# Three moves in a fused attention and hard-swish kernel: one square to ScalarE, one sum of g behind a unit, one square behind an exponential

## The chip, the cores and the metric

The kernel runs on one core of a Trainium2 chip. The metric is the device time of one execution in microseconds (us); the profile's own count, the span, begins with the first instruction of the program and ends with the last. The engines have short names: PE is TensorE (matrix products), DVE is VectorE, ACT is ScalarE, POOL is GpSimd, SP is SyncE, which here only issues DMAs. Each engine works through its own queue in order and waits for the others by semaphores.

## The reference

The computation is cosine attention, followed by a two-layer network with a hard-swish between the layers.

```python
# q, k, v: (8, 12, 448, 64) float32; w_in: (768, 2048); w_out: (2048, 768)
q_n = q / (norm(q, axis=-1) + 1e-06)
k_n = k / (norm(k, axis=-1) + 1e-06)
scores = q_n @ k_n.T / tau
attn = exp(scores - max(scores))
attn = attn / (sum(attn) + 1e-09)
x = (attn @ v).transpose(0, 2, 1, 3).reshape(3584, 768)
h = x @ w_in
g = h * clip(h + 3, 0, 6) / 6
out = g @ w_out                       # float32
```

## The kernel before, in words

The 96 heads are worked on two at a time: 48 pairs, numbered 0 to 47, six to a batch. Raw queries and keys come in "items": item j holds the queries or the keys of two pairs, so that items 2d and 2d+1 belong to pairs 2d and 2d+1. From item 14 on, an even item holds keys and an odd one queries; item 18 is thus the keys of pairs 18 and 19, and item 21 the queries of pairs 20 and 21. An item is 128 partitions by 896 numbers in float32.

What happens to an item: LQ loads it (a DMA on SP's queue), SQ squares it, RE sums the squares (VectorE), NO makes the reciprocals of the norms with four small instructions on ScalarE, NM multiplies them in and casts to bf16 (GpSimd or VectorE), XD transposes by a DMA, and CK and CS copy the keys to where the scores read them (CK on VectorE; CS, from pair 14 on, as two small copies "km" on GpSimd). An SQ may run on ScalarE (letter a, line 227), on GpSimd (p) or on VectorE (v, both line 229). Two buffers hold squares, so the square of item j waits for the reduce of item j-2.

What happens to a pair i: SC.i.g makes four groups of scores. Groups 0 to 2 are two matmuls into two banks of PSUM each (line 445), group 3 is one. EX.i.g takes the exponentials on ScalarE, one instruction for each bank (line 463), and so frees the bank. VA.i.g multiplies by the values (line 486) into the tile PV; FI.i divides by the sums on VectorE (lines 506 and 507) and frees PV for the next pair; XB or XP transposes the result by DMA into xT.

The network is cut into units. A "first product" F is six matmuls (line 597) into one bank; then comes a relu on ScalarE (line 613, it writes one of three tiles u), and a product on VectorE (line 619) that writes g and frees the bank. The second product is done in blocks by a scheme with seven products in place of eight (units such as 5a.3: product 5 of block pair 3, line 762), which need sums of blocks of g (g_sum, line 740, VectorE) and sums of blocks of w_out (weight_sums, WS, line 710, on VectorE or GpSimd). A copy or an addition then reads the bank (lines 781, 787, 799, 810, 819), and GpSimd does additions on what was copied out (lines 791 to 803).

Scores, first products and second products all take their banks in turn from one ring of six: M0, M1, Y, Z, M2, M3. A unit can't start before the sixth-last user's bank was read out.

The order of all engines' work is written by hand. Up to pair 17 it is the list PLAN: a text of steps, each of which puts instructions at the end of the queues of the engines that it uses. U issues the next unit's matmuls, UA its ScalarE step, UV its VectorE step, UP its GpSimd step; W issues the next DMA of weights from GpSimd's queue. From pair 18 on there is one turn for each pair, with its units in TURNS; "+6.3" stands for the sum that product 6 of block pair 3 needs. In a turn, each unit's steps on ScalarE and VectorE follow its matmuls at once; the reduce RE of item i+5 follows the last unit.

The steps that the change touches stand here. In PLAN's line 51, SQ.19 on ScalarE and SQ.18 on GpSimd follow each other; behind them on GpSimd come the two copies of CS.14, then WS.6.p.0 and WS.7.p.0; on VectorE comes WS.1.v.0, which waits for the second of four DMAs of w_out. In PLAN's line 58, SQ.21 on ScalarE stands between EX.16.2 and EX.16.3. In TURNS, turn 29 has four first products, a sum and a product unit; in turn 30, product 2.3 and its sum, and in turn 31, product 6.3, come later.

Of the kernel before, what the change touches and what calls it, by code (L numbers as in the profile page):

```python
# [60 lines left out]
]  # L61
# [3 lines left out]
def kernel(  # L65
# [773 lines left out]
    def products(text):  # L839
# [17 lines left out]
        26: "F 5a.2 4.2 F 2.2",  # L857
        27: "F F 1.2 F 6.2",
        28: "F F 7.2 3.3",
        29: "F F F +6.3 F 5a.3",  # L860
        30: "4.3 F F 2.3 +1.3",
        31: "1.3 F F 6.3 7.3",
        32: "3.4 F F F 5a.4",
# [156 lines left out]
    SC = [psum_s.tile([128, 2, 512], FP32, name=f"SC{n}", tag=f"SC{n}") for n in range(2)]  # L1020
# [118 lines left out]
```

## Time and profile before

| what | value |
|---|---|
| median of three runs | 403.48 us (402.41, 403.48, 406.3) |
| the profiled execution's own time | 403.63 us |
| its span | 401.8 us |
| PE busy | 392.5 us, 98% |
| DVE, ACT, POOL busy | 297.2, 274.5, 248.2 us |
| granted TensorE clock | 1.00 in every stretch |

How to read it: times in the timeline are microseconds from the span's start; each row has the start, the length, the engine, the line of the kernel, the operation and its tiles ("written <- read"), how many instructions it merges, and in brackets how long the engine stood idle before it and what released it. A matmul's record overlaps with its successor's. An instruction's record starts when its engine takes it up; time in which it is blocked further on is part of its length. In the trace, line 51's squares stand at 81.87 (ScalarE) and 82.19 (GpSimd), line 58's at 105.91; the scores of turn 18 begin near 112, those of turn 29 at 192.07 and those of turn 30 at 199.73.

### The profile page before, as it was taken

What the parts mean: (1) busy time and instruction counts of PE and PEld (TensorE: products, weight loads), DVE (VectorE), ACT (ScalarE), POOL (GpSimd) and SP (SyncE); (2) the same over time, 40 slices, a digit from 0 to 9 for tenths busy, and PEclk for the clock granted to TensorE, in tenths of its full rate; (3) what the DMA queues carried; (4) which work ended last, traced back from release to release, by engine and by line L of the source; (5) the groups of instructions that cost most, each with busy time, mean ns of one, the idle gap of its engine ahead of it and who ended that gap; (6) DMA issues with size and microseconds to landing.
All of it is one profiled execution on the core that took longest, in us unless ns stands there. A gap on an engine that the chain in (4) does not pass through costs nothing.

```text
span 401.8 us, 9650 instructions
## 1 busy us (share of the span) xinstructions
PE 392.5 (98%) x3669; PEld 230.9 (57%) x3669; DVE 297.2 (74%) x519; ACT 274.5 (68%) x629; POOL 248.2 (62%) x241
## 2 busy tenths in 40 slices
PE   7999999999999999999999999999999999999996
PEld 5666565545565555555555655555655656555563
DVE  6897688999986697758877767778786566455663
ACT  6899998768997677676776767677677574224230
POOL 7899665591746879698498569839936304201060
PEclk9999999999999999999999999999999999999999
DMA  8999988999479997694866697687665222320143
GB/s 289 293 245 254 232 162 191 246 148 234 97 174 213 192 214 176 145 222 116 208 169 169 171 194 171 155 182 209 124 120 92 46 67 57 74 56 20 29 92 97
DMA packets 92365, 63.73 MB, mean 159 GB/s; under 512 B 56096, under 2 KB 91552, under 8 KB 92320
## 3 DMA queue, kind: packets, MB, share of 16 engines
q1 hardware_dynamic: 87408, 56.45, 60.8%
q0 software_dynamic: 4512, 6.29, 9.4%
q8 instruction: 28, 0.46, 0.5%
q10 hardware_dynamic: 400, 0.39, 0.3%
q14 instruction: 17, 0.14, 0.1%
HBM read 45.61 MB, written 11.01 MB: 141 GB/s over the span
## 4 chain that ended last, share of the span: by engine, by line
PE 77%; DVE 7%; DMA 4%; POOL 4%; issue 3%; ACT 3%; SPq 0%; POOLq 0%; DVEq 0%; ACTq 0%
PE M L597 20%; PE M L762 19%; PE PV L486 10%; PE Y L762 6%; PE Z L762 5%; PE Y L597 5%; PE M L445 5%; PE Z L597 5%; DMA w_out_sb<-in_moe_w_out_dram 2%; DMA big<-in_q_dram 2%; POOL nrm L297 2%; DVE gT L619 2%; POOL big L229 1%; DVE w_sum L710 1%; PE Z L445 1%
## 5 line engine op out<-in xcount | busy, mean ns | idle before, releaser
L597 PE MATMUL M<-xT,w_in_sb 128*128 128x448 bf16 x528 | 111.2, 353 | 0.2 <-ACT at L463 0.2
L597 PEld LDWEIGHTS <-w_in_sb 128*128 128x128 bf16 x768 | 72.4, 98 | 64.3 <-issue 3.1
L463 ACT ACTIVATE at<-M 128x448 bf16<-128x448 f32 x195 | 98.0, 571 | 13.4 <-PE M L445 10.9
L297 POOL TENSOR_TENSOR nrm<-big,r 128x896 bf16<-128x896 f32 (+1 forms) x46 | 76.6, 1671 | 14.4 <-ACT r L260 7.1
L229 POOL TENSOR_TENSOR big<-big 128x896 f32<-128x896 f32 (+3 forms) x41 | 63.3, 1549 | 13.9 <-DVE n L241 5.4
L613 ACT ACTIVATE u<-M 128x448 bf16<-128x448 f32 x88 | 49.3, 561 | 31.3 <-PE M L597 27.8
L486 PEld LDWEIGHTS <-at 128*128 128x128 bf16 (+1 forms) x1536 | 53.9, 97 | 23.3 <-issue 14.4
L619 DVE SCALAR_TENSOR_TENSOR gT<-u,M 128x448 bf16<-128x448 bf16 x75 | 45.8, 617 | 26.0 <-ACT u L613 25.7
L486 PE MATMUL PV<-vx,at 128*128 128x65 bf16 (+1 forms) x1536 | 63.5, 194 | 0.6 <-DVE on L507 0.2
L241 DVE TENSOR_REDUCE n<-big 128x14 f32<-128x896 f32 (+1 forms) x50 | 51.7, 1040 | 2.5 <-POOL big L229 1.5
L762 PEld LDWEIGHTS <-gT 128*128 128x128 bf16 x352 | 33.9, 98 | 23.8 <-issue 0.2
L762 PE MATMUL M<-w_out_sb,gT 128*128 128x384 bf16 x248 | 45.2, 326 | 0.0
L762 PEld LDWEIGHTS <-gs 128*128 128x128 bf16 x312 | 30.1, 98 | 20.8 <-issue 0.6
L791 POOL TENSOR_TENSOR big<-big 128x384 f32<-128x384 f32 x14 | 14.9, 1062 | 36.0 <-ACT big L810 35.9
L402 POOL COPY km<-tT 64x128 bf16<-64x128 bf16 x34 | 13.3, 391 | 38.4 <-DMA tT<-nrm 9.3
L445 PE MATMUL M<-tT,kz 64*128 64x448 bf16 (+1 forms) x172 | 33.5, 351 | 1.2 <-DVE gT L619 0.9
L507 DVE TENSOR_TENSOR on<-PV,rc 128x512 bf16<-128x512 f32 x48 | 33.2, 691 | 1.7
L803 POOL TENSOR_TENSOR o<-o,big 128x384 f32<-128x384 f32 x12 | 12.6, 1056 | 30.6 <-ACT o L799 21.1
L463 ACT ACTIVATE at<-Z 128x448 bf16<-128x448 f32 x52 | 29.5, 567 | 2.0 <-PE M L445 1.8
L463 ACT ACTIVATE at<-Y 128x448 bf16<-128x448 f32 x47 | 26.7, 568 | 4.6 <-PE Z L445 4.3
L597 PE MATMUL Y<-xT,w_in_sb 128*128 128x448 bf16 x132 | 28.7, 353 | 0.0
L762 PE MATMUL M<-w_sum,gs 128*128 128x384 bf16 (+1 forms) x160 | 28.5, 322 | 0.0
(128 smaller groups left out, 581.8 us busy)
## 6 DMA issues: line engine op xcount, KB each, us to landing
big<-in_k_dram SPq DMA_DIRECT2D x24, 448.0 KB, 4.8
big<-in_q_dram SPq DMA_DIRECT2D x24, 448.0 KB, 4.3
out_dram<-o SPq DMA_DIRECT2D x107, 96.0 KB, 2.2
big<-in_v_dram SPq DMA_DIRECT2D x48, 128.0 KB, 4.1
big<-in_v_dram SPq DMA_DIRECT2D x48, 96.0 KB, 4.4
w_out_sb<-in_moe_w_out_dram POOLq DMA_DIRECT2D x4, 768.0 KB, 9.5
w_in_sb<-in_moe_w_in_dram POOLq DMA_DIRECT2D x4, 384.0 KB, 8.3
w_in_sb<-in_moe_w_in_dram POOLq DMA_DIRECT2D x2, 768.0 KB, 10.8
```

The source lines that it names most:

```text
L229: engines[e].tensor_tensor(out=o, in0=i, in1=i, op=ALU.mult)
L241: nc.vector.tensor_reduce(out=n2s[d % 2][:, j % 2, c], in_=sq[:, :, :, :].rearrange("p g c d -> p (g c) d")[:, c, :], axis=AX.X, op=ALU.add,)
L297: engines[e].tensor_tensor(out=nrm[:, :, g, :].rearrange("p c g d -> p g c d"), in0=raw_of[j][:, g, :, :], in1=rs[d % 2][3][:, j % 2, :] . ...
L445: nc.tensor.matmul(o, ks, qt[rows], start=True, stop=True)
L463: nc.scalar.activation(out=o, in_=x, func=AF.Exp, scale=inv_tau)
L486: nc.tensor.matmul(pv_out(j, h), at[rows, n, q_cols(i // HP, j)], vt[rows, 3 + h if name == "M" else 5 * h + int(name[1]), :], start=(name ...
L507: nc.vector.tensor_tensor(out=on[:, :, :, :].rearrange("p j h d -> p h j d"), in0=pv4[:, :, :, 0:D], in1=rc[:, :, :].to_broadcast([128, 2, ...
L597: nc.tensor.matmul(ps[:, 0:S], w_in_sb[:, cc, fc * 128 : (fc + 1) * 128], x[:, cc, 0:S], start=(cc == 0), stop=(cc == CC - 1),)
L613: nc.scalar.activation(out=u[:, :], in_=ps[:, 0:S], func=AF.Relu, bias=0.5, scale=1.0 / 6.0)
L619: nc.vector.scalar_tensor_tensor(out=g[:, fc, c0 : c0 + S], in0=u[:, :], scalar=1.0, in1=ps[:, 0:S], op0=ALU.min, op1=ALU.mult,)
L762: nc.tensor.matmul(m, lhs[:, c, :], rhs[:, c, c0 : c0 + width], start=(base is None and c == 0), stop=(c == KC - 1), skip_group_check=True,)
L791: nc.gpsimd.tensor_tensor(out=e, in0=d, in1=e, op=ALU.add)
```

## The change

Three edits, each in a text that orders the work. The square of item 18 is issued on ScalarE, right behind that of item 19, where it was issued on GpSimd. In turn 29, the sum for product 6.3 follows the fourth first product, where it followed the third. The square of item 21, on ScalarE before and after, follows EX.16.3, where it followed EX.16.2. No instruction is added or taken away beyond the square's change of engine.

```diff
-    "... XD.17 U W U UA UA SQ.19.a.0.7 SQ.18.p.0.7 U CS.14.v WS.1.v.0 UV UV",
+    "... XD.17 U W U UA UA SQ.19.a.0.7 SQ.18.a.0.7 U CS.14.v WS.1.v.0 UV UV",
...
-    "VA.15.1 VA.15.2 EX.16.2 SQ.21.a.0.7 SC.17.0 VA.15.3.h SC.17.1 EX.16.3 FI.15 U VA.16.0 EX.17.0 VA.16.1 UV",
+    "VA.15.1 VA.15.2 EX.16.2 SC.17.0 VA.15.3.h SC.17.1 EX.16.3 SQ.21.a.0.7 FI.15 U VA.16.0 EX.17.0 VA.16.1 UV",
...
-        29: "F F F +6.3 F 5a.3",
+        29: "F F F F +6.3 5a.3",
```

2 rows, old and new, of the table PLAN are left out of this document.

## The prediction

> **What bounds the kernel now.** I read the page's first lines, then the busy time by stretches of 20 us, then the chain of waits in order of time, and last the timeline of each engine at the places that the change touches.
>
> ```profile
> span 401.8 us, 9650 instructions
> PE 392.5 (98%) x3669; PEld 230.9 (57%) x3669; DVE 297.2 (74%) x519; ACT 274.5 (68%) x629; POOL 248.2 (62%) x241
> ```
>
> ```profile
> 80.00:100.00 20.00, 19.56 (x160) 10.31 (x159) 19.79 (x29) 14.99 (x34) 11.27 (x7) 1.00 1.13 192
> 100.00:120.00 20.00, 19.50 (x220) 11.49 (x221) 18.19 (x32) 18.56 (x42) 12.70 (x13) 1.00 0.61 139
> 120.00:140.00 20.00, 20.00 (x172) 11.45 (x170) 13.54 (x25) 14.30 (x37) 14.55 (x16) 1.00 0.95 199
> ...
> 200.00:220.00 20.00, 19.25 (x184) 11.20 (x181) 15.26 (x24) 14.23 (x33) 18.23 (x16) 1.00 0.66 168
> ```
>
> TensorE is the bound: 98% busy, and in 120 to 140 it has no hole (columns: PE, PEld, DVE, ACT, POOL busy, clock, DMA share, GB/s). So only a hole in TensorE's work can be won back, and one that is closed moves all that follows it forward. Holes are left in 80 to 100, 100 to 120 and 200 to 220. By the places given above (turn 29 from 192, its successor from 199.7), all three edits sit at holes. Which engine makes them, the chain tells for the first two:
>
> ```profile
> 81.69 3.02 DVE w_sum L710
> ...
> 106.97 0.70 DVE on L507
> 107.72 1.12 PE PV L486 x32
> ```
>
> From 81.69 to 107.67 the chain runs through VectorE, which is 19.79 of 20 us busy there, and it begins with WS.1.v.0, an addition of 3.02 us.
>
> **Part 1, the square of item 18.** Why does that addition take 3.02 us? Two later ones of the same size stand together as one row of 1.82, 0.91 each. GpSimd's rows beside it tell:
>
> ```profile
> 81.37 0.80 POOL L946 DMA_DIRECT2D w_out_sb<-in_moe_w_out_dram  x1
> 82.19 1.69 POOL L229 TENSOR_TENSOR big<-big 128x896 f32<-128x896 f32 x1
> 83.82 1.38 POOL L402 COPY km<-tT 64x128 bf16<-64x128 bf16 x2
> 85.28 6.15 POOL L710 TENSOR_TENSOR w_sum<-w_out_sb 128x1536 bf16<-128x1536 bf16 x2
> ```
>
> ```profile
> 84.63 0.61 DVE L619 SCALAR_TENSOR_TENSOR gT<-u,Z 128x448 bf16<-128x448 bf16 x1
> 85.16 0.61 DVE L619 SCALAR_TENSOR_TENSOR gT<-u,M 128x448 bf16<-128x448 bf16 x1
> ...
> 98.30 1.82 DVE L710 TENSOR_TENSOR w_out_sb<-w_out_sb 128x1536 bf16<-128x1536 bf16 x2
> ```
>
> The 82.19 row is the square that the change takes off GpSimd. It ends about 83.8; 0.91 later, at 84.71, the addition ends, and only then do the copies behind the square finish. So the addition stood blocked until the square was over, and the copies waited for the addition in turn. Without the square, GpSimd comes from its DMA issue (end 82.17) straight to the two copies. I take it that the addition gets in at the latest after the first copy: both copies take 1.38 less the 0.89 of the addition, 0.49, so one ends by 82.45 and the addition by 83.4. That is 1.3 us earlier. If it gets in at 82.17 it is 1.6; if nothing blocks it from 81.69 on, 2.1. The two additions on GpSimd then start 1.6 earlier and end 1.6 before 91.43 (85.28 + 6.15), so they reach no further against VectorE's moved work than today. What does TensorE get of it?
>
> ```profile
> 83.93 1.30 PE L597 MATMUL Y<-xT,w_in_sb 128*128 128x448 bf16 x6
> 85.29 0.35 PE L445 MATMUL Z<-tT,kz 64*128 64x448 bf16 x1
> ...
> 86.36 1.29 PE L597 MATMUL M<-xT,w_in_sb 128*128 128x448 bf16 x6 [0.19 <-ACT at L463]
> ...
> 89.35 0.35 PE L445 MATMUL M<-tT,kz 64*128 64x448 bf16 x1
> 89.66 0.35 PE L445 MATMUL Y<-tT,kz 64*128 64x448 bf16 x1
> ...
> 90.19 2.43 PE L597 MATMUL M<-xT,w_in_sb 128*128 128x448 bf16 x12
> ...
> 192.26 0.54 PE L445 MATMUL M<-tT,kz 64*128 64x448 bf16 x4
> 192.73 0.66 PE L486 MATMUL PV<-vx,at 128*128 128x65 bf16 x16
> ```
>
> Unhindered, two pairs of scores take 0.47 (192.26 to 192.73), one 0.24. Twelve L597 matmuls step 2.27 (2.43 less the 0.16 by which the last overlaps), six 1.14. So SC.14.0 could start at 83.93 + 1.14 = 85.07 and the next unit at 85.31; it starts at 86.36, 1.05 late, since the banks Z and M2 come free with the products that end at 85.24 and 85.77. At 89.35 two pairs and the next unit could start at 89.82; it starts at 90.19, 0.37 late, on the product of bank Y. Together 1.4, the most that part 1 can give here. A VectorE lead of 1.3 puts the two products' ends at 83.9 and 84.5, before 85.07, so the first hole closes under any of the three leads; the second needs Y's product 0.3 earlier.
>
> Now the added instruction on ScalarE:
>
> ```profile
> 81.87 0.94 ACT L227 ACTIVATE big<-big 128x896 f32<-128x896 f32 x1
> 83.00 0.54 ACT L613 ACTIVATE u<-M 128x448 bf16<-128x448 f32 x1 [0.19 <-PE M L597]
> 85.33 0.54 ACT L613 ACTIVATE u<-M 128x448 bf16<-128x448 f32 x1 [1.79 <-DVE gT L619]
> ...
> 89.17 0.54 ACT L613 ACTIVATE u<-M 128x448 bf16<-128x448 f32 x1 [0.93 <-DVE gT L619]
> ...
> 99.61 0.48 ACT L810 COPY big<-M 128x384 f32<-128x384 f32 x1 [1.02 <-PE M L762]
> ```
>
> It is one square like the 81.87 row, 0.94, right behind it. The relu of 83.00 then starts at 83.7, and 1.79 of idle time behind it swallow the rest; if that cover shrinks, as it does when VectorE is earlier, the relu of 85.33 starts at 84.3, still 1 us earlier than now. So the square costs nothing; were it not covered it would cost 0.94. It waits for no new thing: its data and the reduce of item 16 were there long before. What is late next is ScalarE: behind 89.17 it has no hole of note until 98.6 (99.61 less 1.02). That relu waits for VectorE today; with that gone it waits for TensorE's unit, which is 1.05 to 1.2 earlier. From there the lead of ScalarE, TensorE and VectorE is one and the same, and the chain to 107.72 (FI.14, the normalisations, FI.15) carries it. I take 1.2; bounds 0.9 (second hole stays and a little is lost) and 1.4.
>
> A page of the Trainium skill speaks to the blocking: SBUF — State Buffer, section "Who interferes with whom", says that a VectorE operation with two SBUF inputs and a GpSimd operation that reads SBUF exclude each other for a whole instruction, the first to issue going first, and infers that generating DMA descriptors doesn't block such an operation. By that rule the addition, issued at 81.69 ahead of the square, would have gone first; the row of 3.02 us says otherwise. By the rule the lead would be 2.1 and part 1 would reach its 1.4.
>
> **Part 2, the sum of g in turn 29.** Unit "+6.3" is one VectorE addition (L740).
>
> ```profile
> 198.20 1.69 POOL L297 TENSOR_TENSOR nrm<-big,r 128x896 bf16<-128x896 f32 x1
> ```
>
> ```profile
> 198.44 2.00 DVE L740 TENSOR_TENSOR gs<-gT,big 128x1024 bf16<-128x1024 bf16 x1
> ```
>
> ```profile
> 198.16 0.54 ACT L613 ACTIVATE u<-M 128x448 bf16<-128x448 f32 x1 [0.29 <-PE M L597]
> 199.50 0.48 ACT L799 COPY o<-M 128x384 f32<-128x384 f32 x1 [0.80 <-PE M L762]
> ```
>
> ```profile
> 199.92 0.35 PE L445 MATMUL M<-tT,kz 64*128 64x448 bf16 x2
> 201.02 0.37 PE L445 MATMUL M<-tT,kz 64*128 64x448 bf16 x2 [0.75 <-DVE gT L619]
> 201.32 0.67 PE L486 MATMUL PV<-vx,at 128*128 128x65 bf16 x16
> ```
>
> The sum stands blocked behind GpSimd's normalisation, which ends about 199.85, and is done at 200.44. The product of the last first-product unit waits behind it (to 200.98), though its relu ended at 198.70; SC.30.2 waits for its bank. From 199.92 to 201.32 go 1.40 us where 0.47 would do: 0.93 lost. Moved behind the product, the sum starts near 199.3, still behind the same normalisation, and still ends at 200.44; the product ends near 199.3 and the other bank is copied out by 199.98, before SC.30.2 could start at 200.1. Nothing new waits: the next user, sum 2.3, stands in turn 30, and product 6.3 in turn 31. RE.34, queued behind both, starts 0.5 earlier. No DMA moves. Value 0.9; bounds 0.75 (the wait as the row counts it) and 0.93.
>
> **Part 3, the square of item 21.**
>
> ```profile
> 105.49 0.62 ACT L463 ACTIVATE at<-Y 128x448 bf16<-128x448 f32 x1
> 105.91 1.02 ACT L227 ACTIVATE big<-big 128x896 f32<-128x896 f32 x1
> ```
>
> ```profile
> 106.16 1.46 PE L762 MATMUL Y<-w_sum,gs 128*128 128x384 bf16 x8
> ```
>
> The square and EX.16.3 change places. TensorE's unit at 106.16 waits for the exponential of bank Y ahead of both; then it waits for FI.15 (107.67). EX.16.3 earlier by a square's length meets no one who waits; EX.17.0 starts as before. The square itself comes one exponential later, and its reduce stands behind FI.16, past 107.72. Value 0; bounds: 0.1 gained (107.72 less the unit's end, 106.16 + 1.46), 0.6 lost (one exponential, if someone does wait for the square).
>
> **Sum.** The profiled execution took 403.63 around its span of 401.8, 0.15 over the median 403.48. 403.63 − 1.2 − 0.9 − 0 = 401.5; against the median **401.4 us**, 0.5% faster.
>
> **Rivals.** (a) Part 1 gives nothing: it is the DMA issue or some other hold, not the square, that blocks the addition until 83.8. For it: it wasn't let in between the DMA issue and the square. Against: the end of the square and 0.91 fit to 0.02, and the sum of 198.44 shows the same pattern. Time 403.5 − 0.9 = 402.6. (b) Slower: the addition is passed over at every boundary of GpSimd's queue until the first of its two additions ends. The copies would end at 82.7 and the addition of 3.08 at 85.8, WS.1 at 86.7, 2.0 later than now; both products and SC.14.0 wait for it, so TensorE loses 2.0: 403.5 + 2.0 − 0.9 = 404.6. It decides as soon as WS.1 ends after 84.7. For it: the one time it was passed over. Against: at 83.82 and 199.85 VectorE came in at the first boundary between two computing instructions. (c) The lead is lost later: DMA is 0.95 busy in 120 to 140 and GpSimd 18.23 of 20 in 200 to 220; if a load or a transpose sets the pace, part 1's lead ends in a wait there: 402.6, or 403.5 if part 2's goes too. Against: TensorE waits for neither today, in 20 us without a hole. (d) The edit of turn 29 doesn't help, because SC.30.2 then waits for the other bank: 403.5 − 1.2 = 402.3.
>
> **How the numbers follow.** Forecast 0.62, (a) 0.13, (b) 0.08, (c) 0.12, (d) 0.05. The forecast's own range, from the bounds of the parts, is 401.0 (1.4 + 0.93 + 0.1 off 403.48) to 402.4 (0.9 + 0.75 − 0.6 off) before the scatter of runs; the runs shown lie from 402.41 to 406.3, so 1 below the median is within reach. Low: 401.0 less 0.9 of that scatter, 400.1. High: (a), (d) and (c) in full, 403.6. (b) is left out with a little of each side. Faster by over 1% (about what a measurement of this kernel can tell from no change) would need 399.4, more than all holes named here give, so only scatter: 0.08. Slower by over 1% would need 407.5, more than (b): 0.05 for it with scatter and for the unseen. Within 1%: 0.87.
>
> **What would show it.** Right: WS.1.v.0 takes under 1.8 us and ends by 83.5; the unit after SC.14.0 starts within 0.3 of the pair; the PV row now at 107.72 stands near 106.5; sum 6.3 starts after 199 less the lead and SC.30.2 follows SC.30.1 at once; windows from 120 on stay full. Wrong: WS.1 still ending at 84.7 or later, a hole in TensorE where none is now, or a PV row near 106.5 with the end unmoved.

## The result, and the profile after

| | before | after |
|---|---|---|
| median | 405.0 us (402.41 to 406.93, 16 runs) | 402.69 us (401.29 to 405.3, 16 runs) |
| ratio to before, 95% interval | 1 | 0.9948 [0.9922, 0.9973] |
| span of the profiled execution | 401.8 us | 401.6 us |

The change saves 0.52%, some 2.1 us. The median of before moved from 403.48 to 405.0 with more runs, so the ratio counts, not the difference to 403.48. The two profiled spans are nearly equal. That has to be explained first. Page of after, first lines, and its busy time by stretches (start:end, length, then PE, PEld, DVE, ACT, POOL busy, clock, DMA share, GB/s):

```profile
span 401.6 us, 9649 instructions
PE 392.2 (98%) x3669; PEld 230.8 (57%) x3669; DVE 297.1 (74%) x519; ACT 275.5 (69%) x630; POOL 247.1 (62%) x240
```

```profile
80.00:100.00 20.00, 20.00 (x166) 10.69 (x164) 19.23 (x32) 16.96 (x37) 10.60 (x7) 1.00 1.12 210
100.00:120.00 20.00, 19.50 (x227) 11.47 (x220) 18.22 (x31) 18.57 (x42) 12.70 (x13) 1.00 0.62 142
...
200.00:220.00 20.00, 20.00 (x195) 11.62 (x190) 16.43 (x24) 14.50 (x35) 16.98 (x16) 1.00 0.69 177
220.00:240.00 20.00, 19.82 (x201) 11.79 (x199) 14.89 (x25) 13.32 (x32) 14.95 (x14) 1.00 0.81 191
```

The page shows the square's move: ACT has one instruction more (630 for 629), POOL one less (240 for 241). In 80 to 100 TensorE has gone from 19.56 to 20.00 and in 200 to 220 from 19.25 to 20.00: the two holes are closed. In 100 to 120 it is 19.50 in both. A small hole is new in 220 to 240. What hid the gain in the span stands at the start. Timeline of TensorE in after:

```profile
12.12 0.56 PE L342 MATMUL Z<-ident,nrm 128*128 128x128 bf16 x7 [1.39 <-POOL nrm L297]
...
85.32 1.30 PE L597 MATMUL Y<-xT,w_in_sb 128*128 128x448 bf16 x6
...
86.55 0.36 PE L445 MATMUL M<-tT,kz 64*128 64x448 bf16 x1
86.84 1.31 PE L597 MATMUL M<-xT,w_in_sb 128*128 128x448 bf16 x6
...
107.85 1.12 PE L486 MATMUL PV<-vx,at 128*128 128x65 bf16 x32
...
199.98 0.35 PE L445 MATMUL Y<-tT,kz 64*128 64x448 bf16 x1
200.17 0.54 PE L445 MATMUL M<-tT,kz 64*128 64x448 bf16 x4
200.64 0.66 PE L486 MATMUL PV<-vx,at 128*128 128x65 bf16 x16
```

This execution reached the first-product unit into bank Y at 85.32, where the first trace of before had it at 83.93; the 1.39 us went in the first 13 us, ahead of all three edits. From there the stretches are compared between the same instructions. From unit Y to the PV row it takes 107.85 − 85.32 = 22.53 us, against 107.72 − 83.93 = 23.79: 1.26 won. From the first scores of turn 30 to their PV row it takes 200.64 − 199.98 = 0.66, against 201.32 − 199.73 = 1.59 (199.73 is the start of turn 30's scores given above): 0.93 won. Together 2.2; 1.39 of it went at the start, about half a microsecond in turn 33 (below) and a tenth between 120 and 140, and the rest, 0.2, is what the spans differ by. Part 1's rows in after, of VectorE, GpSimd and ScalarE:

```profile
83.06 0.95 DVE L710 TENSOR_TENSOR w_sum<-w_out_sb 128x1536 bf16<-128x1536 bf16 x1
...
91.53 0.68 DVE L740 TENSOR_TENSOR gT<-gT 128x1024 bf16<-128x1024 bf16 x1
...
103.08 2.88 DVE L297 TENSOR_TENSOR nrm<-big,r 128x896 bf16<-128x896 f32 x2
```

```profile
83.00 0.81 POOL L946 DMA_DIRECT2D w_out_sb<-in_moe_w_out_dram  x1
83.80 0.70 POOL L402 COPY km<-tT 64x128 bf16<-64x128 bf16 x2
...
87.66 3.08 POOL L710 TENSOR_TENSOR w_sum<-w_out_sb 128x1536 bf16<-128x1536 bf16 x1
...
103.32 1.70 POOL L803 TENSOR_TENSOR o<-o,big 128x384 f32<-128x384 f32 x1 [0.72 <-ACT big L810]
```

```profile
83.25 1.78 ACT L227 ACTIVATE big<-big 128x896 f32<-128x896 f32 x2
84.93 1.13 ACT L613 ACTIVATE u<-M 128x448 bf16<-128x448 f32 x2
```

WS.1.v.0 takes 0.95 us for 3.02, GpSimd comes from its DMA issue straight to the copies, and the two squares stand together on ScalarE. It looks like the forecast word for word. The experiments show that it is so only by half.

### The profile page after: what moved, and what is told of

Read it like the earlier page. It is cut to its first block, busy times and chain, and to the rows that moved or that the text cites. A ratio compares the mean times of both kernels' runs of the same rounds, so it can differ in the third digit from the quotient of the medians.

```text
span 401.6 us, 9649 instructions
## 1 busy us (share of the span) xinstructions
PE 392.2 (98%) x3669; PEld 230.8 (57%) x3669; DVE 297.1 (74%) x519; ACT 275.5 (69%) x630; POOL 247.1 (62%) x240
## 4 chain that ended last, share of the span: by engine, by line
PE 83%; DVE 6%; POOL 4%; issue 2%; DMA 2%; ACT 1%; SPq 0%; POOLq 0%; ACTq 0%
PE M L597 24%; PE M L762 18%; PE PV L486 11%; PE Y L762 6%; PE Y L597 6%; PE Z L762 5%; PE M L445 5%; PE Z L597 5%; POOL big L229 2%; PE Z L445 2%; DMA big<-in_k_dram 2%; POOL nrm L297 2%; DVE gT L619 1%; PE Y L445 1%; DVE w_out_sb L710 1%
## 5 line engine op out<-in xcount | busy, mean ns | idle before, releaser
L297 POOL TENSOR_TENSOR nrm<-big,r 128x896 bf16<-128x896 f32 (+1 forms) x46 | 77.9, 1697 | 14.4 <-ACT r L260 7.8
L229 POOL TENSOR_TENSOR big<-big 128x896 f32<-128x896 f32 (+3 forms) x40 | 62.3, 1563 | 18.4 <-DMA big<-in_q_dram 7.6
L402 POOL COPY km<-tT 64x128 bf16<-64x128 bf16 x34 | 12.1, 355 | 38.1 <-DMA tT<-nrm 15.1
```

Source lines behind the costliest of these rows:

```text
L229: engines[e].tensor_tensor(out=o, in0=i, in1=i, op=ALU.mult)
L297: engines[e].tensor_tensor(out=nrm[:, :, g, :].rearrange("p c g d -> p g c d"), in0=raw_of[j][:, g, :, :], in1=rs[d % 2][3][:, j % 2, :] . ...
```

## The experiments

Two stretches are read in every trace: A, from unit Y to the PV row, as above, and B, from the first scores of turn 30 to their PV row. "Rest" is from unit Y to the end of the span. The numbers are starts of TensorE's rows subtracted before rounding, so they can differ by 0.01 from rows subtracted by hand.

| kernel | unit Y at | A | B | rest |
|---|---|---|---|---|
| before, first trace | 83.93 | 23.78 | 1.59 | 317.8 |
| before, second | 85.00 | 23.73 | 1.07 | 317.9 |
| before, third | 85.33 | 23.75 | 1.29 | 317.9 |
| exponential alone (part 3) | 83.89 | 23.74 | 1.29 | 317.6 |
| square on GpSimd behind the copies | 85.81 | 23.75 | 1.69 | 318.2 |
| before, addition held back | 87.04 | 24.22 | 1.53 | 318.6 |
| before, GpSimd held back | 85.68 | 22.91 | 1.29 | 316.8 |
| sum alone (part 2) | 84.33 | 22.81 | 0.66 | 317.1 |
| square alone (part 1) | 83.78 | 22.54 | 1.30 | 316.8 |
| after | 85.32 | 22.54 | 0.66 | 316.3 |
| after, again | 85.31 | 22.54 | 0.66 | 315.9 |
| after and turn 32 | 84.64 | 22.54 | 0.66 | 316.3 |
| after, turn 32, GpSimd held back | 85.50 | 22.54 | 0.66 | 316.2 |
| after, addition held back | 83.88 | 24.33 | 0.66 | 317.9 |

### The three parts, each alone, and all three

The square alone:

```diff
-    "... UA SQ.19.a.0.7 SQ.18.p.0.7 U CS.14.v WS.1.v.0 UV UV",
+    "... UA SQ.19.a.0.7 SQ.18.a.0.7 U CS.14.v WS.1.v.0 UV UV",
```

> Only the square of item 18 goes to ScalarE; turn 29 and the square of item 21 stay as before. Theory (the square on GpSimd blocks WS.1.v.0): WS.1.v.0 takes 0.95 to 1.6 us in place of 3.02, SC.14.0 and the unit behind it follow without a hole, TensorE stands 1.2 us earlier from the PV row of FI.15 on (measured from the first row after the start's waits), the hole of 0.75 to 0.9 in turn 30 stays; about 0.3% faster. Rival (something else holds the addition): WS.1.v.0 stays near 3 us and nothing moves. Rival (the lead is lost later): the lead is there at 108 and is gone in a new hole before 240.

402.9 us, ratio 0.9974 [0.9955, 0.9993], 1.05 us. Stretch A is that of after, B that of before. The PV row stands where the forecast had it, near 106.5. Timeline of TensorE:

```profile
106.31 1.12 PE L486 MATMUL PV<-vx,at 128*128 128x65 bf16 x32
```

So part 1 is worth its 1.2 us.

The sum alone:

```diff
-        29: "F F F +6.3 F 5a.3",
+        29: "F F F F +6.3 5a.3",
```

> Only the sum in turn 29 moves. Theory: from SC.30.1 to the PV row behind SC.30.2 go 0.47 us in place of 1.40, WS.1.v.0 still takes about 3 us and the holes at 85 to 90 stay; 0.2% faster if the 0.9 us is kept to the end. Rival (the lead is lost later): a new hole of about 0.5 us in turn 33, where VectorE's three sums of turn 32 collide with GpSimd's square and normalisation, so 0.1% faster.

404.01 us, ratio 0.9996 [0.9975, 1.0017]. In the trace B falls to 0.66, as in every trace with the edit; in the time nothing is resolved. This trace also has a hole in turn 33 (below), and its stretch A is 22.81 although the square still stands on GpSimd.

The exponential alone:

```diff
-    "VA.15.1 VA.15.2 EX.16.2 SQ.21.a.0.7 SC.17.0 VA.15.3.h SC.17.1 EX.16.3 FI.15 ...",
+    "VA.15.1 VA.15.2 EX.16.2 SC.17.0 VA.15.3.h SC.17.1 EX.16.3 SQ.21.a.0.7 FI.15 ...",
```

> Only the square of item 21 moves behind EX.16.3. Theory: nothing that TensorE waits for moves, TensorE's rows from 104 to 112 keep their distances within 0.05 us, ratio 1.000. Rival (the earlier exponential lets SC.17.2 or the values of pair 16 start earlier, or the later square delays item 21's reduce): a change of 0.1 to 0.6 us in those rows.

404.11 us, ratio 0.9998 [0.9978, 1.0019]; A 23.74, as in before to 0.04. Worth nothing.

All three, a second time:

> All three edits once more, for a second trace of the changed kernel. Theory: TensorE gains 1.2 us between 85 and 90 and 0.8 to 0.9 at turn 30; about 0.5% faster. What is open is the hole of 0.5 us in turn 33 of the first trace: if it comes from the lead (VectorE's sums of turn 32 meet GpSimd's square at the new distance), it is there again; if it comes from a load that landed late by chance (5.6 us after its issue in place of 3.7), it is gone.

401.68 us, ratio 0.9936 [0.9914, 0.9958], 2.6 us by the ratio. Together with 0.9948 that is 2.1 to 2.6; the three alone sum to 0.32%, 1.3 us, each with an interval of 0.2% to either side. By the traces the sum is 1.2 for A and 0.4 to 1.0 for B.

What didn't fit was the sum alone and the exponential alone: in both, with the square on GpSimd, the addition that the prediction had seen blocked was not. Timeline of VectorE, exponential alone:

```profile
81.51 0.95 DVE L710 TENSOR_TENSOR w_sum<-w_out_sb 128x1536 bf16<-128x1536 bf16 x1
```

### Is the block of WS.1.v.0 the rule in before?

Before, again, unchanged:

> The kernel before once more, for a second trace. Theory (race): WS.1.v.0 is either free by the time the DMA issue starts and takes 0.95 us, or is released later by the landing of the w_out load and takes near 3 us; with the holes at 85 to 90 in the second case alone. In the first case the trace says how much of part 1's 1.2 us an execution of before has already.

One run of 404.71 us. WS.1.v.0 takes 0.95 here too. To see whether the 3.02 us of the first trace came of a late start against GpSimd's DMA issue, a small instruction that changes no result (VectorE writes zeros into a buffer of sums that isn't in use) was put ahead of the addition, in before and in after:

```diff
-    "... U CS.14.v WS.1.v.0 UV UV",
+    "... U CS.14.v DL WS.1.v.0 UV UV",
+    "DL": lambda: nc.vector.memset(gs["1"][:, 0:4, :], 0.0),
```

> The kernel before with one more small VectorE instruction (a memset of 512 bf16 in 128 partitions, about 0.27 us, into a tile of sums that is written later) ahead of WS.1.v.0; it changes no result. Theory (a race for the port): in the traces with the square on GpSimd in which WS.1.v.0 took 0.95 us it started 0.06 us after GpSimd's DMA issue, in the one with 3.02 us 0.32 after it; started 0.3 later on purpose it is shut out by the square and ends 0.9 us behind its end, 2.4 to 3 us long, and TensorE has the two holes at 85 to 90 again, 1.0 and 0.3 us. Rival (the 3.02 us came with the late landing of the w_out load that released it, not with the square): 0.95 us long, TensorE's holes at most 0.3.

404.41 us, ratio 0.9995 [0.9966, 1.0024]. Timelines of GpSimd and VectorE in this kernel:

```profile
84.64 0.80 POOL L946 DMA_DIRECT2D w_out_sb<-in_moe_w_out_dram  x1
85.47 1.94 POOL L229 TENSOR_TENSOR big<-big 128x896 f32<-128x896 f32 x1
```

```profile
84.98 0.89 DVE L710 TENSOR_TENSOR w_sum<-w_out_sb 128x1536 bf16<-128x1536 bf16 x1
```

The addition started 0.34 us after the DMA issue, as in the first trace (81.69 after 81.37), and went through in 0.89. It was the square that waited: 1.94 us for 1.69. The theory that a start inside the DMA issue alone puts the addition behind the square has fallen. The same instruction in after:

> The three edits with the same memset ahead of WS.1.v.0. Theory (race against the square, which is gone from GpSimd): WS.1.v.0 starts 0.3 after the DMA issue too, but waits at most for one of the two small copies, under 1.5 us long; no hole at 85 to 90; the time stays at 0.994 of before. Rival (any late start is shut out by whatever GpSimd does next, the copies and the first addition): 3 us or more, holes as in the kernel before, 0.997.

403.38 us, ratio 0.9976 [0.9944, 1.0007]. Timelines of VectorE, GpSimd and ScalarE:

```profile
82.57 0.96 DVE L710 TENSOR_TENSOR w_sum<-w_out_sb 128x1536 bf16<-128x1536 bf16 x1 [0.60 <-DMA w_out_sb<-in_moe_w_out_dram]
...
102.85 3.47 DVE L297 TENSOR_TENSOR nrm<-big,r 128x896 bf16<-128x896 f32 x2
```

```profile
102.57 1.00 POOL L803 TENSOR_TENSOR o<-o,big 128x384 f32<-128x384 f32 x1 [0.20 <-ACT big L810]
```

```profile
97.74 0.62 ACT L316 CAST vx<-big 128x512 bf16<-128x512 f32 x1 [2.11 <-DMA big<-in_v_dram]
```

Here the load of w_out landed late; the addition waited for it and ran unblocked. GpSimd's addition on line 803 then came 0.28 ahead of the two normalisations of items 18 and 19, and these took 3.47 us in place of 2.88. Stretch A is 24.33, longer than before's, with the square on ScalarE. The late addition is not what put VectorE behind: the two merged additions of w_out ahead of FI.14 start 13.24 us after unit Y (97.12 − 83.88), in after 13.16 (98.48 − 85.32). A second late load did. ScalarE waited 2.11 us for a load of v and then copied a bank out late, TensorE waited 0.40 us for that copy, and VectorE's FI.14 waited 0.47 us for TensorE. In before with the added instruction ScalarE has the same wait, 2.00 us, and A is 24.22. So neither of the two kernels tells what a late start of WS.1.v.0 alone costs; whether the added instruction made the load of v late is not known.

### Where the square on GpSimd really costs

Groups of VectorE's instructions by line and shape (count | busy us, mean ns of one | idle us before them) in before, third trace:

```profile
L297 DVE TENSOR_TENSOR nrm<-big,r 128x896 bf16<-128x896 f32 x4 | 6.1, 1532 | 0.0
...
L710 DVE TENSOR_TENSOR w_sum<-w_out_sb 128x1536 bf16<-128x1536 bf16 x4 | 3.8, 947 | 0.0
```

and in after:

```profile
L297 DVE TENSOR_TENSOR nrm<-big,r 128x896 bf16<-128x896 f32 x4 | 5.2, 1327 | 0.0
L710 DVE TENSOR_TENSOR w_sum<-w_out_sb 128x1536 bf16<-128x1536 bf16 x4 | 3.9, 976 | 0.0
```

The additions of w_out are no faster in after; the normalisations are, by 0.9 us. The third run of before was taken to follow this:

> The kernel before a third time. Theory: either WS.1.v.0 is long (near 3 us) and the race at NM.18 is won, as in its first trace, or WS.1.v.0 takes 0.95 us, GS.-1.5 1.2 us, and the race is lost, as in its second; TensorE's time from the unit near 84 to the one near 109 is 25.2 us in both cases, 24.0 in the changed kernel.

One run of 404.99 us. Timelines of VectorE, GpSimd and TensorE:

```profile
91.54 1.27 DVE L740 TENSOR_TENSOR gT<-gT 128x1024 bf16<-128x1024 bf16 x1
...
103.50 3.70 DVE L297 TENSOR_TENSOR nrm<-big,r 128x896 bf16<-128x896 f32 x2
```

```profile
83.73 1.72 POOL L229 TENSOR_TENSOR big<-big 128x896 f32<-128x896 f32 x1
...
89.17 3.09 POOL L710 TENSOR_TENSOR w_sum<-w_out_sb 128x1536 bf16<-128x1536 bf16 x1
...
103.45 1.00 POOL L803 TENSOR_TENSOR o<-o,big 128x384 f32<-128x384 f32 x1 [0.43 <-ACT big L810]
```

```profile
109.09 1.08 PE L486 MATMUL PV<-vx,at 128*128 128x65 bf16 x30 [1.08 <-DVE on L507]
```

Read against the rows of after: the square keeps GpSimd from 83.73 to 85.45 and pushes its two additions of w_out, so that the second ends at 92.26 (89.17 + 3.09) where VectorE reached GS.-1.5, a sum of blocks of g (line 740), at 91.54. That sum needs 1.27 us in place of 0.68. VectorE, now late, reaches the normalisations at 103.50, 0.05 after GpSimd took up line 803; the pair takes 3.70 in place of 2.88, FI.15 is late, and TensorE stands still for 1.08. Up to there this trace was ahead: the last matmuls with the values of pair 15 start 20.01 us after unit Y (105.34 − 85.33), in the first trace of before 21.06 (104.99 − 83.93). The one wait takes that lead away. In after GpSimd's second addition ends at 90.74 (87.66 + 3.08), 0.8 ahead of the sum, and VectorE is at the normalisations 0.24 ahead of line 803, which then takes 1.70.

The test: keep the square on GpSimd, but behind the two copies. WS.1.v.0 then can't be blocked by it at 83; the two additions are pushed all the same.

```diff
-    "... UA SQ.19.a.0.7 SQ.18.p.0.7 U CS.14.v WS.1.v.0 UV UV",
+    "... UA SQ.19.a.0.7 U CS.14.v SQ.18.p.0.7 WS.1.v.0 UV UV",
```

> The kernel before with the square of item 18 kept on GpSimd, but issued behind CS.14's two copies and ahead of GpSimd's two additions of w_out. Rival (what the square costs is that it shuts out WS.1.v.0): WS.1.v.0 0.95 us, and no cost is left, 0.997. Theory (it also pushes GpSimd's two additions, whose end then shuts out the sum GS.-1.5 on VectorE; VectorE comes to NM.18 some 0.5 us later against the rest and loses that race to GpSimd's second addition on line 803): GS.-1.5 takes 1.1 to 1.3 us in place of 0.68, TensorE needs 9.2 us from the product unit near 101 to the one near 109 (8.10 in the first trace of before), and the time is 1.000 of before.

405.31 us, ratio 1.0022 [1.0002, 1.0041]. Timelines of VectorE and TensorE:

```profile
83.42 0.95 DVE L710 TENSOR_TENSOR w_sum<-w_out_sb 128x1536 bf16<-128x1536 bf16 x1
...
92.02 1.26 DVE L740 TENSOR_TENSOR gT<-gT 128x1024 bf16<-128x1024 bf16 x1
...
103.97 3.71 DVE L297 TENSOR_TENSOR nrm<-big,r 128x896 bf16<-128x896 f32 x2
```

```profile
109.56 0.62 PE L486 MATMUL PV<-vx,at 128*128 128x65 bf16 x15 [1.08 <-DVE on L507]
```

No gain: the sum is blocked, the normalisations are late, TensorE loses the same 1.08. It is the square's time in GpSimd's queue that costs, not its place beside WS.1.v.0. The sum tells the two kinds of kernel apart in every later trace: it takes 1.14 to 1.52 us in the seven with the square on GpSimd and 0.68 in the six with it on ScalarE.

The other link, the meeting at 103, by itself: in before, two small GpSimd instructions that change no result hold back line 803.

```diff
-    "CK.17.v SC.16.1 NM.18.v XD.18 NM.19.v XD.19 RE.20 UP UP LV.10 ...",
+    "CK.17.v SC.16.1 NM.18.v XD.18 NM.19.v XD.19 RE.20 PL UP UP LV.10 ...",
+    "PL": lambda: [nc.gpsimd.memset(gs["70"][:, 0:4, :], 0.0) for _ in range(2)],
```

> The kernel before with two memsets on GpSimd (512 bf16 in 128 partitions each, about 1 us together, into a tile of sums that is written later) ahead of its second addition on line 803; the square stays on GpSimd; it changes no result. Theory (lost race at NM.18): GpSimd now comes later than VectorE's NM.18, the two normalisations take 2.9 us in place of 3.7, TensorE needs 8.1 to 8.4 us from the unit near 101 to the one near 109 in place of 9.2, and the kernel is 0.2 to 0.3% faster although work was added. Rival (that stretch is bound by ScalarE's exponentials or by TensorE): 9.2 us stay, 1.000.

403.99 us, ratio 1.0014 [0.9993, 1.0035]. Timelines of GpSimd, VectorE and TensorE:

```profile
103.40 1.11 POOL L987 MEMSET gs<- 128x512 bf16 x2
```

```profile
103.81 2.89 DVE L297 TENSOR_TENSOR nrm<-big,r 128x896 bf16<-128x896 f32 x2
```

```profile
108.59 1.12 PE L486 MATMUL PV<-vx,at 128*128 128x65 bf16 x32 [0.26 <-DVE on L507]
```

In the trace the link holds: with GpSimd busy until 104.51 (103.40 + 1.11) the normalisations, from 103.81 on, are back at 2.89, TensorE's idle time falls from 1.08 to 0.26 and A from 23.75 to 22.91. The time did not follow: 0.8 us less was due and none was measured. What the runs without a trace did at this place is not known. So this last link is shown in traces, not in the time.

### Turn 33, and a better version

Both traces with a hole in turn 33 (after, and the sum alone) show the same pattern; those of after, TensorE, VectorE and GpSimd:

```profile
223.46 0.35 PE L445 MATMUL Z<-tT,kz 64*128 64x448 bf16 x1 [0.18 <-DVE gT L619]
```

```profile
217.67 2.05 DVE L740 TENSOR_TENSOR gT<-gT 128x1024 bf16<-128x1024 bf16 x1
219.64 2.17 DVE L740 TENSOR_TENSOR gs<-gT 128x1024 bf16<-128x1024 bf16 x1
```

```profile
217.33 1.84 POOL L229 TENSOR_TENSOR big<-big 128x896 f32<-128x896 f32 x1 [2.73 <-DMA big<-in_q_dram]
219.14 2.13 POOL L297 TENSOR_TENSOR nrm<-big,r 128x896 bf16<-128x896 f32 x1
```

A load of q landed late, 5.6 us after its issue, so GpSimd's square and normalisation fell on VectorE's sums, and each blocked the other. In the second trace of after the load is as late, 5.9 us, but VectorE's second sum came ahead of the square, and there is no hole. The load took 5.6 to 5.9 us in three traces, after twice and the sum alone, and 3.7 to 4.3 in the eleven others. All three are among the six with the edit of turn 29; the eight without it have neither the late load nor the hole. So the hole depends on how a late load meets the sums, and whether the edit makes the load late stays open. Moving one of turn 32's sums behind its unit, as part 2 does in turn 29, is meant to take it out of the way:

```diff
-        32: "3.4 F F F 5a.4",
+        32: "3.4 F F F +6.4 5a.4",
-        32: sums(4, "756"),
+        32: sums(4, "75"),
```

> The three edits, and in turn 32 the sum for product 6 of block pair 4 behind the last first product too (it stood with the sums for 7 and 5 at the turn's start). Theory: the hole of 0.5 us in turn 33 (two of three traces with the sum of turn 29 moved) is gone whatever GpSimd does, since two sums in place of three stand ahead of the products; up to 0.1% faster than the three edits, 0.993 of before. Rival: the moved sum only delays what comes behind it (the reduce, FI), or the hole is a matter of the late load alone: 0.994 with or without a hole.

402.27 us, ratio 0.9952 [0.9929, 0.9975]: no hole in turn 33 in its trace, and the time of after. The load landed in time in that trace (4.3 us), so it doesn't show what the move does against a late one; and TensorE waits 0.31 us near 132 for VectorE's line 819 instead, so that the rest is 316.3 as in after. With the held-back GpSimd of the experiment above as well:

> The three edits, turn 32's sum for product 6 behind its last first product, and the two memsets on GpSimd. Theory: with the square on ScalarE the race at NM.18 is won in most executions already; the memsets make it safe, 8.1 to 8.4 us from the unit near 101 to the one near 109 in every one; 0.992 to 0.995 of before. Rival: the memsets push GpSimd's later additions against VectorE, and the time is that of the three edits or up to 0.2% more.

402.71 us, ratio 0.9973 [0.9955, 0.9992]. Neither beats the change.

## Why the prediction was right, and where it was not

**Size and sign** were right: 0.5% less was forecast, 0.52% and 0.64% were measured. So "within 1%" holds. Behind that stand a mechanism of part 1 that was luck in its size, and a term of part 2 that was too large.

**Part 1, size right, place wrong.** The term of 1.2 us measured 23.75 − 22.54 = 1.2 in stretch A, and 1.05 in time alone. The step that failed is "So the addition stood blocked until the square was over". It fits the rows of the first trace and of that one alone: in the seven later traces with the square on GpSimd (in one of them behind the copies) the addition took 0.89 to 0.95. There the loss is a later one, in five of the seven: the pushed additions of w_out, the blocked sum near 91.5, the normalisations behind line 803 (in before with the addition held back a late load of v adds to it). In the sum alone the meeting at 103 fell out well by chance, and A was 22.81; in the kernel with GpSimd held back it was made to. The first trace could not show this. Its timeline of VectorE has

```profile
91.43 0.68 DVE L740 TENSOR_TENSOR gT<-gT 128x1024 bf16<-128x1024 bf16 x1
```

VectorE, held up by WS.1.v.0, came to this sum 7.50 us after unit Y (91.43 − 83.93), just as GpSimd's additions ended (85.28 + 6.15 = 91.43). In the third trace it is there after 6.21 (91.54 − 85.33), and the additions end after 6.93 (92.26 − 85.33). Both ways cost TensorE the same to a few hundredths (A 23.78 and 23.75), and so the one trace gave the right size for the wrong place: that is luck, not foresight. Of the 1.2 us, 0.84 is the meeting at 103 (A 23.75 against 22.91 with GpSimd held back) and the other 0.37 is still lost when that meeting goes well; in the time the 0.84 was not found. Why the addition was blocked in the first trace stays open: a late start beside the DMA issue doesn't do it (0.89), a late load without the square doesn't either (0.96); a late load with the square on GpSimd could not be produced at will and was not tried.

**The rule weighed in part 1.** The Trainium skill, "SBUF — State Buffer", section "Who interferes with whom", infers that a VectorE operation with two SBUF inputs and the generating of DMA descriptors use different interfaces of the port that the two engines share, so that neither blocks the other, and says that the first to issue goes first. The prediction set the one row of 3.02 us against it. The later traces side with the page: additions of 0.89 to 0.95 us run beside DMA issues of 0.80, and where the addition started 0.34 into the issue it was the square behind that took longer, 1.94 in place of 1.69. Against unit Y the addition ends 2.1 us earlier in after than in the first trace of before (84.01 − 85.32 = −1.31; 84.71 − 83.93 = 0.78): that is the lead that the prediction worked out for the rule, not its own 1.3. TensorE's gain is 1.26 of the 1.4 it named as the most. By the rule the loss had to be sought at another place, and there it was. The 3.02 us remain an exception that no run here explains.

**The square on ScalarE costs nothing**, as said. Against unit Y the relu behind it starts at 84.93 − 85.32 = −0.39, where it was 83.00 − 83.93 = −0.93: 0.54 later, 0.7 was forecast. Unit M at 86.84 follows its pair by 0.29, so nobody waited for it.

**Part 2, right mechanism, a little too large.** The rows of after, VectorE and GpSimd:

```profile
198.98 0.62 DVE L619 SCALAR_TENSOR_TENSOR gT<-u,M 128x448 bf16<-128x448 bf16 x1 [0.21 <-ACT u L613]
199.52 1.27 DVE L740 TENSOR_TENSOR gs<-gT,big 128x1024 bf16<-128x1024 bf16 x1
```

```profile
198.55 1.69 POOL L297 TENSOR_TENSOR nrm<-big,r 128x896 bf16<-128x896 f32 x1
```

The product goes first, the sum waits behind GpSimd's normalisation (1.27 us), and the third pair of scores (in the merged 200.17 row) follows at once. But 0.93 is what this one trace lost. Over the eight traces without the edit B is 1.07 to 1.69, mean 1.38, so the edit is worth 0.4 to 1.0, mean 0.7. The term was sized by a single draw of how the sum and the normalisation meet.

**Part 3** is worth nothing, as said. The half microsecond that TensorE lacks in 100 to 120 is still missing with all three edits (19.50 of 20): the edit wins none of it.

**The rivals.** (a) did not happen: part 1 brought its 1.2. Its doubt whether the square held WS.1.v.0 in the first trace stays open; the DMA issue, its suspect, held no addition up in twelve later traces. (b), the addition passed over until GpSimd's own are done, did not happen in any trace. (c) is half there: the leads lasted to the end (rest 315.9 to 316.3 against 317.9), but half a microsecond of them went in turn 33 in one trace of after, by a late load. (d) did not happen: the pairs of turn 30 follow without a gap.

## What to carry to other kernels

A block between VectorE and GpSimd in one trace shows what can happen, not what does: take a second trace of the same kernel before building on it, and compare between the same instructions, since the start alone moved by 2 us here, once by 3. An instruction taken off GpSimd is worth what stands behind it in the queue: follow GpSimd's later instructions to the places where they meet VectorE's additions and normalisations, even 20 us on. Where two instructions that block each other start within a tenth of a microsecond, a lead of a few tenths for the engine that feeds TensorE decides which of them pays. And before a delay is put down to the instruction that was moved, count from a fixed instruction whether it is still there: here a late load of v did what a late addition seemed to do.

## What the runs showed of the hardware

- Five hundredths of a microsecond can decide a meeting. With GpSimd's line 803 ahead by 0.05 (103.45 to 103.50) the two normalisations took 3.70 us in place of 2.88 and TensorE lost 1.08; with VectorE ahead by 0.24, line 803 took 1.70 in place of 1.00 and TensorE lost nothing. Below that the records don't tell the order. In the sum alone GpSimd's row starts 0.03 ahead, and still it is GpSimd that waits (VectorE, then GpSimd):

```profile
102.37 2.88 DVE L297 TENSOR_TENSOR nrm<-big,r 128x896 bf16<-128x896 f32 x2
```

```profile
102.34 1.97 POOL L803 TENSOR_TENSOR o<-o,big 128x384 f32<-128x384 f32 x1 [0.44 <-ACT big L810]
```

- Unit Y was reached between 83.78 and 85.81 us in 13 of the 14 traces and at 87.04 in one, in kernels that are nearly alike up to there. That is as much as the whole change is worth, and it comes in the first microseconds: in after, one wait for a normalised item takes 1.39 us (the row of 12.12), and 0.28 in the first trace of before.
